# A nine-group Strassen output product: the turn of the next q in the following group's MLP phase, one subtraction on VectorE, second-half stores behind the turns of x

## The chip, the cores and the metric

The kernel runs on one core of a Trainium2 chip. The metric is the device time of one execution in microseconds (us); the smaller the better. TensorE is called PE, VectorE DVE, ScalarE ACT, GpSimd POOL and SyncE SP, as the profile names them. SP computes nothing here: it issues nearly all of the DMAs, in the order in which they are written.

## What is computed

Attention over 8 batches, 8 heads, 576 tokens and head size 64, with k and v averaged over blocks of 8 tokens (72 keys are left), and behind it an MLP on all 4608 tokens, 512 to 2048 to 512, with `g = h - tanh(h)` in the middle.

```python
k_p = k.reshape(B, H, Sp, pool, D).mean(axis=3)
v_p = v.reshape(B, H, Sp, pool, D).mean(axis=3)
scores = scale * np.matmul(q, k_p.transpose(0, 1, 3, 2))
attn = softmax(scores)                      # over the 72 pooled keys
attn_out = np.matmul(attn, v_p)
x = attn_out.transpose(0, 2, 1, 3).reshape(B * S, H * D)
h = x @ w_in
out = (h - np.tanh(h)) @ w_out
```

## The kernel before

The MLP goes over nine groups g = 0 to 8 of 512 tokens. Beside the MLP of group g runs the attention of batch nb = g + 1, and beside that the loading and pooling of batch nn = g + 2. A batch has 576 tokens, a group 512, so group g + 1 needs only the first blocks of batch g + 1: blocks 0 to 2 (of 128 tokens) for the groups 2 and 3, blocks 0 and 1 for the groups 4 and 5, block 0 for the group 6.

A group from 1 on has two phases. The **MLP phase** (lines 910 to 923) makes h for 16 slices of 128 hidden units from `xT`, the turned (transposed) x: eight matmuls for a pair of slices (`h_pair`, line 514), tanh of it on ACT (526), the difference to it on DVE (527, into `Gt`), and on DVE the sums `P`, `Q` that Strassen's scheme wants. The **product phase** (925 to 942) has seven products of eight steps each, in 14 half products u = 0 to 13 (line 562). They add up in two PSUM banks, C1 and C2, and `after_product` takes partial sums off: m4, m45, m451 are ACT copies of C1 at three points (594, 600, 607); POOL forms m4 - m45 (601) and m451 - m45 (608); DVE finishes with 605 and 610 into the output tile `O`. Between the half products stand the scores of batch nb (u = 0 to 4, line 333, exp on ACT, 352) and attention times values (`av`, u = 6, 7, 8, 9, 11, one block each: line 380 on PE, 397 and 398 on DVE into `x_sb`). SP then issues a DMA transpose that turns the block into `xT` (line 418).

At u = 7 POOL pools k (233 to 241, into `kd`) and v (251 to 275) of batch nn and casts q to `q_bf` (183, 187); then SP is given five DMA transposes that turn `q_bf` into `qT` (193). In the next MLP phase (p = 1 in group 1, p = 4 in later ones) SP turns `kd` into `kT` (316), POOL places that in `KB` (284 to 288), and SP issues the loads of the batch after (lines 137 to 170).

The order is written by hand (`tc.manual_schedule()`): each engine's instructions, and SP's DMAs, run in the order of the code, and an instruction that waits holds all that stand behind it on its engine. `store` (577) puts half a group's output on SP's queue: `store(g, 1)` behind product 5, `store(g, 0)` at the group's end.

Of the kernel before, what the change touches and what calls it, by code (L numbers as in the profile page):

```python
# [12 lines left out]
ALU = mybir.AluOpType  # L13
# [14 lines left out]
NG = T // TG  # L28
# [14 lines left out]
def kernel(  # L43
# [9 lines left out]
    nc = tc.nc  # L53
# [52 lines left out]
    m45 = const.tile([128, 2, HD], FP32, name="m45")  # L106
    m451 = const.tile([128, 2, HD], FP32, name="m451")
# [71 lines left out]
    def q_cast(b, eng=nc.gpsimd.tensor_copy, parts=1):  # L179
        t = q_raws.pop(b)  # L180
        n = H // parts
        for h in range(0, H, n):
            eng(  # L183
                out=q_bf[:, 0:R, h : h + n, :].rearrange("p j h d -> p h j d"),
                in_=t[:, h : h + n, 0:R, :],
            )
        eng(out=q_bf[:QT, R, :, :], in_=t[:QT, :, R, :])

    def q_dma_transpose(b):
        qT = work.tile([128, NHP, S], BF16, name="qT", tag="qT")  # L190
        for j in range(R + 1):
            rows = 128 if j < R else QT
            nc.sync.dma_start_transpose(  # L193
                out=qT[:, :, j * 128 : j * 128 + rows],
                in_=q_bf[:rows, j, :, :].rearrange("p h d -> p (h d)"),
            )
        qTs[b] = qT
# [84 lines left out]
    def kb_main(kb, ps, t0, t1, engs):  # L282
        kv = kb.rearrange("p (t x) -> p t x", x=KP)
        engs[0](out=kv[0:D, t0:t1, 0:G], in_=ps[0:D, :, 0:G])  # L284
        engs[1](out=kv[D:128, t0:t1, G:128], in_=ps[D:128, :, G:128])  # L285

    def kb_left(kb, ps, eng):
        eng(
            out=kb[D:128, :].rearrange("p (t x) -> p t x", x=KP)[:, :, 128 : 128 + LO],
            in_=ps[D:128, 0 : NM * LO].rearrange("p (x t) -> p t x", t=NM),  # L290
        )
# [22 lines left out]
    def k_dma_transpose(b):  # L314
        kT = work.tile([128, NT, 128], BF16, name="kT", tag="kT", bufs=1)
        nc.sync.dma_start_transpose(
            out=kT[:, :, :], in_=kdups.pop(b)[:, :, :, :].rearrange("p t a d -> p (t a d)")
        )
        kTs[b] = kT

    def k_place(b, eng):
        kT = kTs.pop(b)
        kb_main(KB[b % 2], kT[:, 0:NM, :], 0, NM, (eng, eng))
        kb_left(KB[b % 2], kT[:, NM, :], eng)
# [115 lines left out]
    def out_segments(c0, nrows):  # L440
        segs = []
        r = 0
        while r < nrows:
            c = c0 + r
            bb = c // S
            i = c % S
            if i < QA:
                j = i // 128
                p0 = i % 128
                ln = min(128 - p0, nrows - r, QA - i)  # L450
                dst = out[bb * S : bb * S + QA, :].rearrange("(p j) m -> p j m", j=R)[
                    p0 : p0 + ln, j, :
                ]
            else:
                ln = min(S - i, nrows - r)
                dst = out[bb * S + i : bb * S + i + ln, :]
            segs.append((r, r + ln, dst))
            r += ln
        return segs
# [62 lines left out]
    def h_pair(g, p, b0, ts):  # L522
        h_mms(g, p, PS[:, b0, :])
        h_mms(g, p + NP, PS[:, b0 + 1, :])
        t2 = TS[:, 2 * ts : 2 * ts + 2, :]
        nc.scalar.activation(out=t2, in_=PS[:, b0 : b0 + 2, :], func=ACT.Tanh)  # L526
        nc.vector.tensor_sub(out=Gt[:, p, :, :], in0=PS[:, b0 : b0 + 2, :], in1=t2)  # L527

    def h_one(g, p, s, b0, ts):
        h_mms(g, p + s * NP, PS[:, b0, :])  # L530
        nc.scalar.activation(out=TS[:, ts, :], in_=PS[:, b0, :], func=ACT.Tanh)
        nc.vector.tensor_sub(out=Gt[:, p, s, :], in0=PS[:, b0, :], in1=TS[:, ts, :])  # L532

    def sum_p(a, b):
        nc.vector.tensor_tensor(  # L535
            out=P[:, a:b, :], in0=Gt[:, a:b, 0, :], in1=Gt[:, a:b, 1, :], op=ALU.add
        )

    def sum_q(a, b):
        nc.vector.tensor_tensor(  # L540
            out=Q[:, a:b, :], in0=Gt[:, a:b, 0, 0:HT], in1=Gt[:, a:b, 1, HT:TG], op=ALU.add
        )

    def sum_d(a, b):
        nc.vector.tensor_tensor(  # L545
            out=Dg[:, a:b, :, :],
            in0=Gt[:, a:b, :, 0:HT],
            in1=Gt[:, a:b, :, HT:TG],
            op=ALU.subtract,
        )  # L550
# [8 lines left out]
    def product(bk, lhs, rhs, k0, k1, first):  # L559
        for k in range(k0, k1):  # L560
            for tt in range(2):
                nc.tensor.matmul(  # L562
                    PS[:, bk, tt * HD : (tt + 1) * HD],
                    lhsT=lhs(k, slice(tt * 128, (tt + 1) * 128)),
                    rhs=rhs[:, k, :],
                    start=(first and k == 0 and tt == 0),
                    stop=(k == NP - 1),
                    skip_group_check=True,
                )

    def chain(bk):
        return PS[:, bk, :].rearrange("p (t n) -> p t n", t=2)

    def store(g, th, tts=(0, 1), c0=0, c1=DM):
        for tt in tts:
            for n, (r0, r1, dst) in enumerate(out_segments(g * TG + th * HT + tt * 128, 128)):
                nc.sync.dma_start(out=dst[:, c0:c1], in_=O[r0:r1, 2 * th + tt, c0:c1])
# [14 lines left out]
    def after_product(g, n):  # L592
        if n == 0:
            nc.scalar.copy(out=m4, in_=chain(C1))
        if n == 1:
            nc.vector.tensor_tensor(out=O[:, 2:4, 0:HD], in0=chain(C2), in1=m4, op=ALU.add)
            sum_d(0, 2)
            sum_d(2, 4)
        if n == 2:
            nc.scalar.copy(out=m45, in_=chain(C1))  # L600
            nc.gpsimd.tensor_tensor(out=m4, in0=O[:, 2:4, 0:HD], in1=m45, op=ALU.subtract)  # L601
            sum_d(4, 6)
            sum_d(6, 8)
        if n == 3:
            nc.vector.tensor_tensor(out=O[:, 0:2, HD:DM], in0=m4, in1=chain(C2), op=ALU.subtract)
        if n == 4:
            nc.scalar.copy(out=m451, in_=chain(C1))
            nc.gpsimd.tensor_tensor(out=m451, in0=m451, in1=m45, op=ALU.subtract)  # L608
        if n == 5:
            nc.vector.tensor_tensor(  # L610
                out=O[:, 2:4, HD:DM], in0=m451, in1=chain(C2), op=ALU.subtract
            )
            store(g, 1)

    v_bf = (
        v_raw[0]
# [64 lines left out]
    for m, base, step, cm in (  # L681
# [6 lines left out]
            out=m,  # L688
# [7 lines left out]
    for i in range(2):  # L696
# [4 lines left out]
        out=spread.rearrange("p (t x) -> p t x", x=32)[:, :, 0:LO],  # L701
# [200 lines left out]
    def next_loads(b):  # L902
        load_k(b)
        load_v(b)
        load_q(b)

    for g in range(1, NG):
        nb = g + 1 if g + 1 < B else None
        nn = g + 2 if g + 2 < B else None
        for p in range(NP - 1):  # L910
            h_pair(g, p, (0, 2, 4, 6, 0, 2, 4)[p], p % 2)
            if p >= 4:
                sum_p(2 * p - 8, 2 * p - 6)
            if nb is not None and p == (1 if g == 1 else 4):
                k_dma_transpose(nb)
                k_place(nb, nc.gpsimd.tensor_copy)
                if nn is not None:
                    next_loads(nn)
        h_one(g, NP - 1, 1, 0, 2)
        h_one(g, NP - 1, 0, 1, 3)  # L920
        sum_p(6, 8)
        sum_q(0, 4)
        sum_q(4, 8)
        ps_a = Banks(2, 3, 4, 5, 0, 1)
        for u in range(14):
            n, half = u // 2, u % 2
            bk, lhs, rhs = products[n]
            if n == 6 and g == NG - 1:
                break
            product(bk, lhs, rhs, 4 * half, 4 * half + 4, n < 2)  # L930
            if half:
                after_product(g, n)
            if nb is not None:
                if u < NT:
                    scores(nb, u)
                if u in (6, 7, 8, 9, 11):
                    av(nb, (6, 7, 8, 9, 11).index(u), ps_b1, True)
                if u == 7 and nn is not None:
                    pool_k(nn, nc.gpsimd)
                    pool_v(nn, nc.gpsimd)  # L940
                    q_cast(nn)
                    q_dma_transpose(nn)
        if g < NG - 1:
            nc.scalar.copy(out=O[:, 0:2, 0:HD], in_=chain(C1))
            store(g, 0)
    store(NG - 1, 0, c0=HD)
    for tt, c0, c1, eng in (
        (0, 0, HD, nc.scalar.copy),
# [45 lines left out]
```

## Time and profile before

| | us |
|---|---|
| median of 3 runs | 382.73 (381.8 to 384.0) |
| the profiled execution | 385.25 |
| its span, first to last instruction | 383.5 |
| PE busy | 293.2 (76% of the span) |
| DVE, ACT, POOL busy | 221.6, 140.4, 139.1 |
| mean granted PE clock, as a share of full speed | 0.897 |

Times in rows are us from the span's start. The share of busy time is a mean over stages with different limits, so the stages have to be looked at one by one.

### The profile page before, as it was taken

What the parts mean: (1) busy time and instruction counts of PE and PEld (TensorE: products, weight loads), DVE (VectorE), ACT (ScalarE), POOL (GpSimd) and SP (SyncE); (2) the same over time, 40 slices, a digit from 0 to 9 for tenths busy, and PEclk for the clock granted to TensorE, in tenths of its full rate; (3) what the DMA queues carried; (4) which work ended last, traced back from release to release, by engine and by line L of the source; (5) the groups of instructions that cost most, each with busy time, mean ns of one, the idle gap of its engine ahead of it and who ended that gap; (6) DMA issues with size and microseconds to landing.
All of it is one profiled execution on the core that took longest, in us unless ns stands there. A gap on an engine that the chain in (4) does not pass through costs nothing.

```text
span 383.5 us, 5441 instructions
## 1 busy us (share of the span) xinstructions
PE 293.2 (76%) x2029; PEld 181.8 (47%) x2048; DVE 221.6 (58%) x389; ACT 140.4 (37%) x225; POOL 139.1 (36%) x126
## 2 busy tenths in 40 slices
PE   7899987699019991099944988199927899999991
PEld 2544553269004680045831476046812486485580
DVE  5766689686015970138903883249704875883860
ACT  4565730661004620036311642046212543623510
POOL 7307079207900079110593029701791111011030
PEclk9999999699758997579985999679986999999998
DMA  7999994921046920488103696158705505103004
GB/s 255 204 249 307 236 317 115 291 83 28 0 96 150 314 63 0 89 237 267 25 5 62 160 308 93 38 139 277 167 0 78 147 5 135 37 0 111 0 2 109
DMA packets 66538, 49.84 MB, mean 130 GB/s; under 512 B 40016, under 2 KB 53456, under 8 KB 66512
## 3 DMA queue, kind: packets, MB, share of 16 engines
q1 hardware_dynamic: 59104, 42.94, 42.5%
q0 software_dynamic: 4752, 4.72, 7.4%
q10 hardware_dynamic: 2656, 1.84, 1.8%
q8 instruction: 16, 0.26, 0.3%
q14 instruction: 10, 0.08, 0.1%
HBM read 36.70 MB, written 9.44 MB: 120 GB/s over the span
## 4 chain that ended last, share of the span: by engine, by line
PE 40%; POOL 23%; DVE 14%; DMA 10%; issue 4%; SPq 4%; ACT 3%; POOLq 0%; ACTq 0%; DVEq 0%
PE PS L514 19%; PE PS L562 14%; DVE Gt L527 6%; POOL v_raw L251 4%; POOL k_raw L233 4%; DMA w1b<-in_moe_w_in_dram 4%; SPq L193 3%; DMA k_raw<-in_k_dram 3%; DVE P L535 3%; ACT TS L526 2%; POOL q_bf L183 2%; PE PS L333 2%; DMA xT<-x_sb 2%; PE PS L496 2%; POOL k_raw L238 2%
## 5 line engine op out<-in xcount | busy, mean ns | idle before, releaser
L514 PE MATMUL PS<-xT,w1b 128*128 128x512 bf16 x496 | 124.7, 410 | 72.7 <-DMA xT<-x_sb 34.7
L514 PEld LDWEIGHTS <-w1b 128*128 128x128 f16 x512 | 53.0, 104 | 141.8 <-issue 54.7
L527 DVE TENSOR_TENSOR Gt<-PS,TS 128x1024 bf16<-128x1024 f32 x56 | 68.3, 1222 | 55.9 <-ACT TS L526 55.8
L526 ACT ACTIVATE TS<-PS 128x1024 f32<-128x1024 f32 x56 | 57.3, 1025 | 117.3 <-PE PS L514 116.7
L601 POOL TENSOR_TENSOR m<-O,m 128x512 f32<-128x512 f32 x8 | 10.9, 1366 | 111.9 <-DVE Dg L545 67.5
L610 DVE TENSOR_TENSOR O<-m,PS 128x512 f32<-128x512 f32 x8 | 5.5, 688 | 67.8 <-POOL m L608 67.2
L562 PE MATMUL PS<-w2b,Gt 128*128 128x256 f16 x256 | 33.6, 273 | 1.2 <-DVE Gt L532 1.0
L562 PE MATMUL PS<-w2b,P 128*128 128x256 f16 x256 | 32.3, 273 | 0.0
L398 DVE TENSOR_TENSOR x_sb<-PS,rden 128x256 bf16<-128x256 f32 x72 | 30.6, 425 | 2.5
L284 POOL COPY KB<-kT 64x288 bf16<-64x288 bf16 x6 | 2.8, 470 | 80.0 <-DMA kT<-kd 80.0
L233 POOL TENSOR_TENSOR k_raw<-k_raw 128x1280 f32<-128x1280 f32 x7 | 20.3, 2896 | 27.8 <-DMA k_raw<-in_k_dram 27.8
L562 PE MATMUL PS<-w2s,Dg 128*128 128x256 f16 x240 | 28.5, 273 | 0.0
L562 PEld LDWEIGHTS <-Gt 128*128 128x128 bf16 x256 | 24.3, 98 | 7.4 <-DVE Gt L532 2.9
L562 PEld LDWEIGHTS <-P 128*128 128x128 bf16 x256 | 24.6, 98 | 4.7 <-issue 1.4
L352 ACT ACTIVATE E<-PS 128x288 bf16<-128x288 f32 x60 | 21.4, 411 | 10.6 <-PE PS L333 10.6
L562 PEld LDWEIGHTS <-Dg 128*128 128x128 bf16 x240 | 23.0, 98 | 2.6 <-issue 0.2
L535 DVE TENSOR_TENSOR P<-Gt 128x1024 bf16<-128x1024 bf16 x32 | 22.1, 692 | 0.3
L545 DVE TENSOR_TENSOR Dg<-Gt 128x1024 bf16<-128x1024 bf16 x32 | 21.0, 719 | 0.0
L380 PE MATMUL PS<-VB,E 128*128 128x130 bf16 x240 | 20.2, 220 | 0.1
L333 PE MATMUL PS<-qT,KB 128*128 128x288 bf16 (+5 forms) x128 | 17.0, 289 | 2.4 <-POOL KB L285 2.3
L380 PEld LDWEIGHTS <-E 128*128 128x128 bf16 x240 | 16.8, 98 | 1.9 <-issue 0.4
L251 POOL TENSOR_TENSOR v_raw<-v_raw 128x1280 f32<-128x1280 f32 x6 | 17.3, 2881 | 0.0
(107 smaller groups left out, 353.0 us busy)
## 6 DMA issues: line engine op xcount, KB each, us to landing
k_raw<-in_k_dram SPq DMA_DIRECT2D x7, 1024.0 KB, 5.9
q_raw<-in_q_dram SPq DMA_DIRECT2D x7, 1024.0 KB, 9.9
v_raw<-in_v_dram SPq DMA_DIRECT2D x7, 1024.0 KB, 8.7
out_dram<-O SPq DMA_DIRECT2D x36, 128.0 KB, 2.4
out_dram<-O SPq DMA_DIRECT2D x16, 256.0 KB, 2.7
w1b<-in_moe_w_in_dram POOLq DMA_DIRECT2D x4, 512.0 KB, 15.0
w2b<-in_moe_w_out_dram POOLq DMA_DIRECT2D x4, 512.0 KB, 17.5
k_raw<-in_k_dram SPq DMA_DIRECT2D x7, 128.0 KB, 5.9
```

The costliest lines, as they stand in the source:

```text
L233: first = eng.tensor_tensor(out=r[:, :, 0:4, :], in0=r[:, :, 0:4, :], in1=r[:, :, 4:8, :], op=ALU.add)
L251: eng.tensor_tensor(out=r[:, :, 0:4, :], in0=r[:, :, 0:4, :], in1=r[:, :, 4:8, :], op=ALU.add)
L333: nc.tensor.matmul(dst[p : p + w], lhsT=KB[b % 2][:, o : o + w], rhs=qTs[b][:, m, c0:c1], start=True, stop=True,)
L352: nc.scalar.activation(out=E[:, t, half * hs : (half + 1) * hs], in_=ps[:, :], func=ACT.Exp, scale=SCALE)
L380: nc.tensor.matmul(ps[:, 2 * n : 2 * n + 2, :].rearrange("p h d -> p (h d)") if n < 2 else ps.rearrange("p (a s) d -> p a s d", s=2)[:, :, ...
L398: nc.vector.tensor_tensor(out=x_sb[:, half, :, :], in0=ps[:, :, 0:D], in1=rden[:, :, :].to_broadcast([128, 4, D]), op=ALU.mult,)
L514: nc.tensor.matmul(dst, lhsT=w1b[:, fb, i * 128 : (i + 1) * 128], rhs=xT[:, fb, c0 : c0 + TG], start=(fb == 0), stop=(fb == NFB - 1),)
L526: nc.scalar.activation(out=t2, in_=PS[:, b0 : b0 + 2, :], func=ACT.Tanh)
L527: nc.vector.tensor_sub(out=Gt[:, p, :, :], in0=PS[:, b0 : b0 + 2, :], in1=t2)
L535: nc.vector.tensor_tensor(out=P[:, a:b, :], in0=Gt[:, a:b, 0, :], in1=Gt[:, a:b, 1, :], op=ALU.add)
L545: nc.vector.tensor_tensor(out=Dg[:, a:b, :, :], in0=Gt[:, a:b, :, 0:HT], in1=Gt[:, a:b, :, HT:TG], op=ALU.subtract,)
L562: nc.tensor.matmul(PS[:, bk, tt * HD : (tt + 1) * HD], lhsT=lhs(k, slice(tt * 128, (tt + 1) * 128)), rhs=rhs[:, k, :], start=(first and k ...
```

## The change

Three edits. The five turns of q leave the end of the pooling block at u = 7 and stand in the next group's MLP phase, behind the turn of k (for g > 1; the first batch that is turned this way, 2, keeps its place ahead of the loop). The subtraction m451 - m45 goes from POOL to DVE. `store(g, 1)` moves from behind product 5 to behind u = 12, so behind the last turn of x; for the last group it stands behind the loop.

```diff
         if n == 4:
             nc.scalar.copy(out=m451, in_=chain(C1))
-            nc.gpsimd.tensor_tensor(out=m451, in0=m451, in1=m45, op=ALU.subtract)
+            nc.vector.tensor_tensor(out=m451, in0=m451, in1=m45, op=ALU.subtract)
         if n == 5:
             nc.vector.tensor_tensor(
                 out=O[:, 2:4, HD:DM], in0=m451, in1=chain(C2), op=ALU.subtract
             )
-            store(g, 1)
@@
             if nb is not None and p == (1 if g == 1 else 4):
                 k_dma_transpose(nb)
+                if g > 1:
+                    q_dma_transpose(nb)
                 k_place(nb, nc.gpsimd.tensor_copy)
                 if nn is not None:
                     next_loads(nn)
@@
                     pool_k(nn, nc.gpsimd)
                     pool_v(nn, nc.gpsimd)
                     q_cast(nn)
-                    q_dma_transpose(nn)
+            if u == 12:
+                store(g, 1)
         if g < NG - 1:
             nc.scalar.copy(out=O[:, 0:2, 0:HD], in_=chain(C1))
             store(g, 0)
+    store(NG - 1, 1)
     store(NG - 1, 0, c0=HD)
```

SP's queue from the product phase of group 1 to the loads in group 2, before (L193 turns q, L418 turns x, L577 stores, L316 turns k, L137 and L146 load k):

```order
L418 DMA_TRANSPOSE xT<-x_sb 128x4x128 x2
L193 DMA_TRANSPOSE qT<-q_bf 128x4x128 x4
L193 DMA_TRANSPOSE qT<-q_bf 128x4x64
L418 DMA_TRANSPOSE xT<-x_sb 128x4x128 x2
L577 DMA out_dram<-O 64x512 x4
L418 DMA_TRANSPOSE xT<-x_sb 128x4x64
L577 DMA out_dram<-O 64x512 x4
L316 DMA_TRANSPOSE kT<-kd 128x5x128
L137 DMA k_raw_86<-in_k_dram 128x4x512
L146 DMA k_raw_86<-in_k_dram 64x1x512
```

and the same stretch now:

```order
L418 DMA_TRANSPOSE xT<-x_sb 128x4x128 x4
L418 DMA_TRANSPOSE xT<-x_sb 128x4x64
L577 DMA out_dram<-O 64x512 x8
L316 DMA_TRANSPOSE kT<-kd 128x5x128
L193 DMA_TRANSPOSE qT<-q_bf 128x4x128 x4
L193 DMA_TRANSPOSE qT<-q_bf 128x4x64
L137 DMA k_raw_86<-in_k_dram 128x4x512
L146 DMA k_raw_86<-in_k_dram 64x1x512
```

All five turns of x now stand ahead of the turns of q, and the turns of q stand directly ahead of the loads. On POOL, before, the subtraction (L608, m_82 is m451) stood between the cast of q and the placing of k:

```order
L183 CAST q_bf<-q_raw 128x8x4x64
L187 CAST q_bf<-q_raw 64x512
L608 TENSOR_TENSOR m_82<-m_82,m_81 128x512
L284 COPY KB_91<-kT 64x4x72
L285 COPY KB_91<-kT 64x4x56
```

On DVE it now stands ahead of the fourth block of attention (L397, L398) of the same product phase:

```order
L398 TENSOR_TENSOR x_sb<-PS,rden 128x256
L608 TENSOR_TENSOR m_82<-m_82,m_81 128x512
L397 RECIPROCAL rden<-PS 128x4
L398 TENSOR_TENSOR x_sb<-PS,rden 128x256
L397 RECIPROCAL rden<-PS 128x4
L398 TENSOR_TENSOR x_sb<-PS,rden 128x256
L610 TENSOR_TENSOR O<-m_82,PS 128x2x256
```

L610, which reads it, no longer depends on POOL's queue.

## Rows read from the trace of the kernel before

**Rows 1.** Waits, whole span: engine line waited for, us in total, times, longest.
```profile
DVE O L610 <- POOL m L608: 67.2, 7, 12.7
...
PE PS L514 <- DMA xT<-x_sb: 34.7, 2, 17.4
...
PE PS L514 <- DVE x_sb L398: 29.2, 3, 9.7
```
**Rows 2.** Busy time by stretch: PE, PEld, DVE, ACT, POOL, clock, DMA share, GB/s.
```profile
144.80:162.20 17.40, 0.02 (x2) 0.01 (x1) 1.72 (x5) 0.59 (x1) 9.91 (x8) 0.58 0.21 41
162.20:179.00 16.80, 16.53 (x63) 7.01 (x66) 8.85 (x9) 7.67 (x8) 0.97 (x3) 0.82 0.94 266
...
321.20:335.00 13.80, 13.70 (x64) 6.27 (x65) 8.79 (x9) 8.23 (x9) 0.00 (x0) 1.00 0.34 83
```
**Rows 3.** Timeline of SP's queue: start us, us, what; groups 1, 2 and 4.
```profile
89.72 2.88 SPq L418 DMA_TRANSPOSE xT<-x_sb  x2
104.39 6.43 SPq L193 DMA_TRANSPOSE qT<-q_bf  x5
110.91 2.52 SPq L418 DMA_TRANSPOSE xT<-x_sb  x2
113.53 3.69 SPq L577 DMA_DIRECT2D out_dram<-O  x4
...
121.14 1.31 SPq L316 DMA_TRANSPOSE kT<-kd  x1
...
219.30 0.58 SPq L137 DMA_DIRECT2D k_raw<-in_k_dram  x1
```
**Rows 4.** Timeline of POOL, groups 0, 1 and 8; idle before in brackets.
```profile
65.56 1.72 POOL L257 TENSOR_TENSOR v_raw<-v_raw 128x320 f32<-128x320 f32 x1
...
88.11 1.27 POOL L601 TENSOR_TENSOR m<-O,m 128x512 f32<-128x512 f32 x1 [18.15 <-DVE Dg L545]
...
95.41 2.88 POOL L251 TENSOR_TENSOR v_raw<-v_raw 128x1280 f32<-128x1280 f32 x1
...
99.98 0.86 POOL L257 TENSOR_TENSOR v_raw<-v_raw 128x320 f32<-128x320 f32 x1
...
104.31 0.61 POOL L187 CAST q_bf<-q_raw 64x512 bf16<-64x512 f32 x1
...
368.24 1.96 POOL L601 TENSOR_TENSOR m<-O,m 128x512 f32<-128x512 f32 x1 [21.84 <-ACT m L600]
```
**Rows 5.** Timeline of PE, groups 1, 2 and 6.
```profile
80.24 1.04 PE L562 MATMUL PS<-w2b,Gt 128*128 128x256 f16 x8
81.11 0.41 PE L333 MATMUL PS<-qT,KB 128*128 128x288 bf16 x2
...
94.16 1.91 PE L562 MATMUL PS<-w2s,Dg 128*128 128x256 f16 x16
113.40 0.61 PE L514 MATMUL PS<-xT,w1b 128*128 128x512 bf16 x1 [17.33 <-DMA xT<-x_sb]
...
306.67 0.42 PE L333 MATMUL PS<-qT,KB 128*128 128x288 bf16 x2 [1.16 <-POOL KB L285]
```
**Rows 6.** Chain that ended last, in order of time, at group 1's last q turn.
```profile
109.62 1.20 SPq L193
```
**Rows 7.** Landing: page's DMA issues; then x's turn at 230.3 alone (ns min/median/max).
```profile
k_raw<-in_k_dram SPq DMA_DIRECT2D x7, 1024.0 KB, 5.9
...
qT<-q_bf SPq DMA_TRANSPOSE x30, 2.5
...
L418 SPq DMA_TRANSPOSE xT<-x_sb x1: 1234/1234/1234, 230.3 to 230.3; - x1
...
DMA to landing us min/median/max: 4.6/4.6/4.6
```
**Rows 8.** Timeline of DVE: last of block 3 in group 2; sums in group 8.
```profile
142.21 0.42 DVE L398 TENSOR_TENSOR x_sb<-PS,rden 128x256 bf16<-128x256 f32 x1
...
366.59 2.49 DVE L545 TENSOR_TENSOR Dg<-Gt 128x1024 bf16<-128x1024 bf16 x4
```

## The prediction

> **What bounds the kernel now.** I read the waits first, then the busy time by stretch, then the queues at the places that these two name. The waits [rows 1] show two stalls of one family. PE waits 34.7 us, in two pieces of 17.4, at the first h matmul of a group for turned x; and 29.2 us, three pieces of 9.7, for DVE to free a bank in line 398. DVE itself waits 67.2 us at line 610 for POOL's subtraction. The stretches [rows 2] show what such a stall costs twice: in the 17.4 us behind group 2's products PE is as good as idle, and the granted clock is 0.58 on the mean, so the lower of its two levels, 1.2 GHz, for most of it; the next MLP phase takes 16.8 us at 0.82, where group 7's, which follows its products without a gap, takes 13.8 at 1.00. So there are five stalls, behind groups 1 to 5, and each is also paid in clock.
>
> The queues say why. In group 1 POOL starts on line 601 at 88.11 and ends the cast of q at 104.9 [rows 4], 16.8 us later. SP has issued two turns of x by 92.6 and then stands at the turns of q until 104.39; these take 6.4 us to issue, and the other turns of x follow at 110.91 [rows 3]. Block 2 is needed for the next group, so PE, done at 96.07, starts at 113.40 [rows 5]. In groups 3 to 5 the needed blocks lie ahead of the turns of q, but line 608 stands behind the cast in POOL's queue, line 610 behind it in DVE's, and block 4's reciprocals and the next group's subtractions behind that.
>
> **The change, part by part.** *Turns of q.* Five issues of 6.4 us leave the place ahead of block 2's turn. In group 1 the third turn of x is then issued at 92.6 and lands 2.5 later, by the turns of q, which are the same instruction on the same shape [rows 7]: 95.1, before PE is done at 96.07. The 17.3 us stall goes. What is late next is the scores of the next group, since they need all of qT: their first step needs the last turn.
>
> Group 2 then starts at 96.07. With 13.8 us of MLP phase [rows 2] its products start at 109.9, and PE comes to the scores 0.87 later (80.24 to 81.11 [rows 5]), at 110.75. The turns of q cannot be earlier than now: the cast ends at 104.9, the last turn is issued at 109.62 [rows 6] and lands at about 111.9, taking 2.3 us for this half-size one (2.5 is the upper end). So PE waits 1.2 us, and I call 111.9 the time S of group 2.
>
> From there the loop is: S, the start of that first step's second half, lies 0.2 us behind the step's start, half of its 0.41, so at 81.3 in group 1, and line 601 starts at 88.11 [rows 4, 5]: 6.8 us. Line 601 to the last turn's landing is 111.9 - 88.11 = 23.8. One round: 30.6 us. PE's own round is 96.07 - 81.11 = 15.0 for the products behind the scores, 13.8 and 0.87: 29.6. So POOL's chain and the turns, not PE, set the pace, by 1.0 us.
>
> *Subtraction on DVE.* About 1.3 us go from POOL (line 601 is the same operation on the same shape [rows 4]), behind the cast, where nobody would now wait for them. It adds one f32 subtraction of 128x512 to DVE, ahead of block 3's reciprocals. Its price on DVE is about 0.6 us (a bf16 difference of twice as many elements takes 2.49/4 = 0.62 [rows 8]), an estimate, and twice that at the worst; block 3 is done at 142.63 in group 2 [rows 8] and its two banks are wanted at 144.8, so 2.2 us are covered. No row shows an f32 subtraction on DVE with both inputs in SBUF, beside POOL or alone. The nearest: line 601 took 1.96 us while DVE formed the differences Dg, and 1.27 otherwise [rows 4, 8], so the two hold each other up by about 0.7. Bounds: nothing for POOL, or 0.7 in each of five chains; and for DVE nothing, or a POOL instruction in flight of up to 2.88 [rows 4], which would be 0.7 or so beyond the cover. I take 0.7 on POOL and nothing beyond the cover, since rows 4 and 8 show just that pair at work.
>
> The Trainium skill has a rule for this (SBUF — State Buffer, "Who interferes with whom"): a DVE instruction with two SBUF inputs and a POOL instruction that reads SBUF exclude one another, and the second to start waits for the whole of the first. Rows 4 and 8 agree for a bf16 pair, no row shows the f32 one; by the rule the sum is the 315 below, without it 312.
>
> *Stores.* `store(g, 1)`'s four issues (3.7 us at most [rows 3]) come behind block 4's turn. Ahead of the turns of q SP now has block 4's turn (1.3), five to eight stores (0.9 each by the slowest row) and the turn of k (1.3). Block 4 is ready at S + 15.0 at the latest, when PE ends its products, so SP is free between S + 22.2 and S + 25.0; the cast frees the turns at S + 6.8 + 16.3 = S + 23.1 (88.11 to 104.39), or 23.8 with the 0.7. I take nothing; the bounds are 0 and 1.9 us a group, and 0 is nearer, since eight stores is the most that any group has.
>
> *Loads.* They stand behind the turns of q now, so they start 1.1 us ahead of S. POOL wants k 8 us behind S (6.8 and line 601), v 6 us later still (95.41 against 89.4 [rows 4]) and q last; k takes 5.9 to land [rows 7], so it is there at S + 5. I take nothing; the cover is 3 us.
>
> *Turns of x behind the loads.* In group 4 the loads started at 219.30, and the turn of x at 230.3 took 4.6 us to land instead of 2.5, at 234.9, 15.6 us behind the loads' start [rows 3, 7]. Now the loads start at S - 1.1 in groups 2 to 5, so block 0 lands at S + 14.5, blocks 1 and 2 at the spacing of SP's issues, 1.26 each, at 15.8 and 17.0. PE ends its products at S + 15.0. Group 3, which needs block 2, starts 2.0 us late: a round of 15.0 + 2.0 + 13.8 + 0.87 = 31.7. Groups 4 and 5, with two blocks, start 0.8 late: 30.5, which is hidden under the round that POOL sets. (The bounds are 2.5 us of landing, no cost at all, and the second rival.)
>
> **The sum.** S of group 2: 111.9 + 0.7 = 112.6. Four rounds lead to S of group 6, one of 31.7 and three of 30.6 + 0.7 = 31.3: 238.2. From there to the end nothing of weight changes: 383.5 - 306.67 = 76.8 [rows 5]. Span 315.0. The profiled execution was 1.75 longer than its span, so 316.8, and the median of the runs stands to it as 382.73 to 385.25: **315**. Without the 0.7 the span is 312.2 (111.9, 31.7, three of 30.6, 76.8), the time 312.
>
> **The rivals.**
>
> *PE alone sets the pace* (turns and POOL faster than I read): S of group 2 at 110.75, rounds of 29.6, span 306.0, time 306. Against it: the 16.8 us are POOL instructions back to back, and the 6.4 us are SP's own issue time.
>
> *The turns of x come late.* For it: the 4.6 us [rows 7] with loads on the queue; and now it is so in every group from 2 to 5. If each of these groups' followers starts 2.5 us late and the clock falls for a part of it (I take 15.3 for the MLP phase, midway between the 13.8 and 16.8 of rows 2), a round is 15.0 + 2.5 + 15.3 + 0.87 = 33.7: S of group 6 at 247.4, span 324.2, time 324. It decides from a start that is 1.6 us late. The Trainium skill (DMA: Bandwidth & Descriptors, "Queues, rings and completion order") says that one queue's descriptors are taken in ring order on each engine, so the turns wait for all that SP issued before; the 4.6 us agrees.
>
> *POOL is held up by DVE throughout: slower than before.* The pooling ran while DVE stood still at line 610; now it runs beside DVE's work. Line 257 took 1.72 us instead of 0.86 while DVE formed sums of weights [rows 4]. Were all of the 16.8 us doubled, S of group 2 would be 128.7, a round 47.4, the span 395, time 394. It decides from a stretch of 14.5 us a chain (five chains against the 72 us gained). Against it: line 251, 2.88 us at 95.41 [rows 4], and most of the chain are work of the MLP phase's first two thirds, where DVE has its reads from PSUM; the sums of two SBUF tensors that rows 4 and 8 show to hurt come behind the chain's end.
>
> *Only half works*: if the turns of x are still held by something in SP's queue, the two 17.3 us stalls stay and three of 9.7 go: 383.5 - 29.1 = 354, time 353.
>
> **How the numbers follow.** Forecast (310 to 319, with the bounds of the subtraction and the stores) 0.68, PE alone 0.10, turns of x late 0.17, half 0.03, POOL doubled 0.02. The range 306 to 325 leaves out the late end of the second rival, the last two and half of the first, in all less than 0.2. Faster by over 0.5%, which is about what can be told from no change, in all cases but the last: 0.97; slower 0.02; the same 0.01.
>
> **What would show it.** Right: no wait of line 514 for x over 2 us; no wait of line 610 for POOL; groups 2 to 6 at 31 us from scores to scores, with a wait of about 1 us for qT in line 333 at u = 0; PE's clock near 1.0 from group 2 on. Wrong: rounds of 33 or more with line 514 waiting for x (second rival); pooling rows longer than before by more than 1 us a chain (third); SP issuing the turns of q later than POOL's cast by more than 0.2 us (the store term).

## The result

The changed kernel takes 317.98 us (median of 4 runs, 316.82 to 319.41) against 382.68 before: a ratio of 0.831, 95% interval 0.8265 to 0.8353. The prediction was 315 with a range of 306 to 325; the span of the profiled execution is 315.1 us where the sum gave 315.0. That the two spans agree to 0.1 us is luck: two misses of some 3 us cancel, an opening that was 3.0 us shorter and rounds that were 3.3 us longer in sum.

The page of the changed kernel, its busy time and the granted clock in 40 slices:

```profile
PE 284.5 (90%) x2048; PEld 180.0 (57%) x2048; DVE 232.9 (74%) x397; ACT 140.5 (45%) x225; POOL 130.9 (42%) x118
...
PEclk9999999989999999999999997999999999999997
```

DVE's wait for POOL at line 610 [rows 1] is not among the waits any more. What is left around the MLP phase, from the waits of the changed kernel (us in total, times, longest):

```profile
PE PS L333 <- DMA qT<-q_bf: 5.7, 4, 2.1
...
PE PS L514 <- DVE x_sb L398: 5.0, 2, 3.4
DVE x_sb L398 <- DMA xT<-x_sb: 3.9, 2, 2.8
```

PE's timeline holds the whole course. These are, for the groups 2 to 6, the first matmul of the MLP phase (L514) and the first scores that had to wait for q (L333); group 5 has no wait there:

```profile
92.87 13.98 PE L514 MATMUL PS<-xT,w1b 128*128 128x512 bf16 x64
...
109.82 0.28 PE L333 MATMUL PS<-qT,KB 128*128 128x288 bf16 x1 [1.98 <-DMA qT<-q_bf]
...
124.72 13.97 PE L514 MATMUL PS<-xT,w1b 128*128 128x512 bf16 x64 [0.33 <-DMA xT<-x_sb]
...
141.76 0.30 PE L333 MATMUL PS<-qT,KB 128*128 128x288 bf16 x1 [2.07 <-DMA qT<-q_bf]
...
158.02 13.97 PE L514 MATMUL PS<-xT,w1b 128*128 128x512 bf16 x64 [1.68 <-DVE x_sb L398]
...
173.16 0.30 PE L333 MATMUL PS<-qT,KB 128*128 128x288 bf16 x1 [0.17 <-DMA qT<-q_bf]
...
191.10 15.66 PE L514 MATMUL PS<-xT,w1b 128*128 128x512 bf16 x64 [3.36 <-DVE x_sb L398]
...
207.47 0.41 PE L333 MATMUL PS<-qT,KB 128*128 128x288 bf16 x2
...
222.27 13.98 PE L514 MATMUL PS<-xT,w1b 128*128 128x512 bf16 x64
...
238.71 0.30 PE L333 MATMUL PS<-qT,KB 128*128 128x288 bf16 x1 [1.47 <-DMA qT<-q_bf]
```

Where before had an idle PE for twice 17.4 us and three times 9.7 [rows 1], there is nothing, 0.3, 1.7, 3.4 and nothing. From S to S (the second half of the first scores, so 207.67 in group 5) the rounds are 31.9, 31.4, 34.5 and 31.0 us; before, the five distances from group 1's scores to group 6's were 42 to 50. PE waits for q at the scores in four groups. The sum had four too, but not the same: it had none in group 3, which waited 2.1 us, and one of some 0.8 us in group 5, which had none. The third round is longer because the MLP phase behind group 4 starts 3.4 us late and then runs at the lower clock of 1.2 GHz for a while: the stretches (busy times, clock, DMA share, GB/s) of that phase and of the next group's, which started on time, are

```profile
191.10:206.60 15.50, 15.50 (x64) 6.67 (x65) 9.35 (x12) 7.66 (x8) 6.66 (x9) 0.89 0.57 134
222.30:236.10 13.80, 13.80 (x67) 6.26 (x65) 10.02 (x14) 8.24 (x9) 10.42 (x10) 1.00 0.56 132
```

The 1.7 us that the lower clock costs did not follow every such wait: in the experiments below, the same phase took 15.66 us behind a wait of 2.2 us (the subtraction from PSUM), and 13.97 behind one of 3.1 us (the cast first). What decides it was not tried.

The late start is the turn of x. The row names line 398, but that line itself waited for block 0's buffer, that is for the same turn. The issue (in ns) and the landing (in us) of block 0's turn behind the loads, in group 2 and then in group 4:

```profile
L418 SPq DMA_TRANSPOSE xT<-x_sb x1: 1257/1257/1257, 118.0 to 118.0; - x1
...
DMA to landing us min/median/max: 5.7/5.7/5.7
```

```profile
L418 SPq DMA_TRANSPOSE xT<-x_sb x1: 2598/2598/2598, 181.4 to 181.4; - x1
...
DMA to landing us min/median/max: 9.2/9.2/9.2
```

In group 3 it is 7.5 us, in group 5 3.6. [rows 7] had 4.6 for group 4 of before. That was not the only turn of x behind loads there: those of groups 2, 3 and 5, issued 16.0, 20.6 and 12.2 us behind the loads' start, took 2.6, 4.3 and 3.0 us, and the 4.3 came 6 us after the last load had landed. So the 4.6 us were no clean measure of what loads ahead of a turn cost.

The pace of the other rounds is POOL's chain and the turns. In group 1, line 183 is the part of the cast that the first four turns of q read; it ends at 101.69 and the turns start at 102.24:

```profile
99.80 1.89 POOL L183 CAST q_bf<-q_raw 128x2048 bf16<-128x2048 f32 x1
```

```profile
102.24 6.44 SPq L193 DMA_TRANSPOSE qT<-q_bf  x5
```

### The profile page after: what moved, and what is told of

It is laid out like the page before. It is cut to its first block, busy times and chain, and to the rows that moved or that the text cites. A ratio compares the mean times of both kernels' runs of the same rounds, so it can differ in the third digit from the quotient of the medians.

```text
span 315.1 us, 5444 instructions
## 1 busy us (share of the span) xinstructions
PE 284.5 (90%) x2048; PEld 180.0 (57%) x2048; DVE 232.9 (74%) x397; ACT 140.5 (45%) x225; POOL 130.9 (42%) x118
## 4 chain that ended last, share of the span: by engine, by line
PE 35%; POOL 22%; DMA 14%; DVE 13%; SPq 6%; issue 4%; ACT 2%; POOLq 0%; DVEq 0%; ACTq 0%
PE PS L562 18%; PE PS L514 9%; SPq L193 6%; DVE Gt L527 6%; DMA xT<-x_sb 4%; DMA w1b<-in_moe_w_in_dram 4%; POOL v_raw L251 4%; POOL k_raw L233 4%; DMA k_raw<-in_k_dram 3%; PE PS L333 3%; DMA qT<-q_bf 3%; PE PS L496 3%; POOL q_bf L183 2%; DVE w2b L553 2%; DVE P L535 2%
## 5 line engine op out<-in xcount | busy, mean ns | idle before, releaser
L514 PE MATMUL PS<-xT,w1b 128*128 128x512 bf16 x512 | 115.2, 386 | 12.3 <-DVE Gt L527 5.4
L514 PEld LDWEIGHTS <-w1b 128*128 128x128 f16 x512 | 50.5, 99 | 74.4 <-issue 14.2
L398 DVE TENSOR_TENSOR x_sb<-PS,rden 128x256 bf16<-128x256 f32 x72 | 30.6, 425 | 6.3 <-DMA xT<-x_sb 3.9
L233 POOL TENSOR_TENSOR k_raw<-k_raw 128x1280 f32<-128x1280 f32 x7 | 20.3, 2897 | 27.7 <-DMA k_raw<-in_k_dram 16.8
L333 PE MATMUL PS<-qT,KB 128*128 128x288 bf16 (+5 forms) x128 | 17.7, 289 | 5.8 <-DMA qT<-q_bf 5.7
L545 DVE TENSOR_TENSOR Dg<-Gt 128x1024 bf16<-128x1024 bf16 x32 | 22.0, 751 | 0.0
L380 PEld LDWEIGHTS <-E 128*128 128x128 bf16 x240 | 16.8, 98 | 1.9 <-issue 0.4
L607 ACT COPY m<-PS 128x512 f32<-128x512 f32 x8 | 4.7, 586 | 29.5 <-PE PS L562 29.5
L562 PE MATMUL PS<-w2s,Q 128*128 128x256 f16 x128 | 16.3, 273 | 0.0
```

Of the source, the lines that this page charges most:

```text
L233: first = eng.tensor_tensor(out=r[:, :, 0:4, :], in0=r[:, :, 0:4, :], in1=r[:, :, 4:8, :], op=ALU.add)
L333: nc.tensor.matmul(dst[p : p + w], lhsT=KB[b % 2][:, o : o + w], rhs=qTs[b][:, m, c0:c1], start=True, stop=True,)
L380: nc.tensor.matmul(ps[:, 2 * n : 2 * n + 2, :].rearrange("p h d -> p (h d)") if n < 2 else ps.rearrange("p (a s) d -> p a s d", s=2)[:, :, ...
L398: nc.vector.tensor_tensor(out=x_sb[:, half, :, :], in0=ps[:, :, 0:D], in1=rden[:, :, :].to_broadcast([128, 4, D]), op=ALU.mult,)
L514: nc.tensor.matmul(dst, lhsT=w1b[:, fb, i * 128 : (i + 1) * 128], rhs=xT[:, fb, c0 : c0 + TG], start=(fb == 0), stop=(fb == NFB - 1),)
L545: nc.vector.tensor_tensor(out=Dg[:, a:b, :, :], in0=Gt[:, a:b, :, 0:HT], in1=Gt[:, a:b, :, HT:TG], op=ALU.subtract,)
```

## The experiments

Ten runs follow. Times are compared with the changed kernel, which ran again in the first set at 318.52 us (316.97 to 319.31), and with the kernel before, at 383.3 to 383.6 beside them.

> The changed kernel once more, as the measure for the three beside it and for how much the opening (all ahead of group 1's products) varies: 77.2 us in the profile of the change, 80.2 in that of before. Time 318 +- 1.5.

It did: 318.52. Over the twelve profiles of this study the same opening code reaches group 1's products after 77.2 to 80.2 us, so 3 us of any comparison of two single profiles can be the opening.

**Each edit alone.** First the turns of q alone: the changed kernel with

```diff
-            nc.vector.tensor_tensor(out=m451, in0=m451, in1=m45, op=ALU.subtract)
+            nc.gpsimd.tensor_tensor(out=m451, in0=m451, in1=m45, op=ALU.subtract)
@@ n == 5
+            store(g, 1)
@@ u == 12, and behind the loop
-                store(g, 1)
-    store(NG - 1, 1)
```

> The first edit alone: the turns of q behind the turn of k in the next MLP phase; the subtraction stays on POOL and the stores behind product 5. Theory: line 610 then waits for POOL's whole chain as before (12 to 13 us in each of groups 1 to 5), DVE holds the bank of block 4 and the next group's subtractions, so each of the five rounds is about 42 us (before: 49, 50, 43, 42, 43) instead of 31: time 364 to 371. Rival: the turns of q alone were the stall, and the subtraction is a small matter: 318 to 325.

Measured: 366.4 us (one run). The waits of this kernel:

```profile
DVE O L610 <- POOL m L608: 67.2, 7, 12.7
PE PS L514 <- DVE x_sb L398: 47.4, 5, 9.7
```

The wait at line 610 is to the tenth what it was [rows 1], and PE now pays it in all five groups instead of three: 9.7 us at most, also where it had stood 17.4 for turned x. Then the subtraction alone: the kernel before with

```diff
-            nc.gpsimd.tensor_tensor(out=m451, in0=m451, in1=m45, op=ALU.subtract)
+            nc.vector.tensor_tensor(out=m451, in0=m451, in1=m45, op=ALU.subtract)
```

> The second edit alone: the subtraction on DVE, the turns of q and the stores where they were. Theory: the turns of x for block 2 still stand behind the turns of q, so the two 17 us stalls behind groups 1 and 2 stay; in groups 3 to 5 the wait of 9.7 us goes, but the turn of k still stands behind the turns of q, the rest of x and the stores in SP's queue, some 38 us behind the scores, and the next scores wait for it instead: nearly nothing is gained, 376 to 383. Rival, as in the prediction's last one: the three waits of 9.7 us go and nothing takes their place: 352 to 358.

Measured: 387.4 us (one run; the kernel before 382.1 to 385.2 beside it). Nothing is gained, and it lies a little above what was expected. PE's timeline and SP's queue at the end of group 3:

```profile
111.37 0.61 PE L514 MATMUL PS<-xT,w1b 128*128 128x512 bf16 x1 [17.64 <-DMA xT<-x_sb]
...
219.28 0.66 PE L333 MATMUL PS<-qT,KB 128*128 128x288 bf16 x2 [12.36 <-POOL KB L285]
```

```profile
200.91 6.41 SPq L193 DMA_TRANSPOSE qT<-q_bf  x5
207.41 2.52 SPq L418 DMA_TRANSPOSE xT<-x_sb  x2
...
215.65 1.32 SPq L316 DMA_TRANSPOSE kT<-kd  x1
```

The stall of 17.6 us for turned x is there, twice. Where DVE had held PE, PE now runs its MLP phase early and stands 12.4 us at the scores for KB: the turn of k is issued at 215.65, behind the turns of q, and nothing has moved that. So the gains do not add: 17 us for one edit, none for the other, 65 for both. Each takes away one of two waits that overlap, and PE then stands at the other one.

**The stores.** `store(g, 1)` behind product 5 again:

```diff
@@ n == 5
+            store(g, 1)
@@ u == 12, and behind the loop
-                store(g, 1)
-    store(NG - 1, 1)
```

> The change without its third edit: the stores of the second half stand behind product 5 again, ahead of block 4's turn. My theory: SP has the same issues to make by the time that the cast of q is done, line 610 no longer waits for POOL, and block 4 isn't needed for the next group, so the edit is worth nothing: within 1 us of the changed kernel (317 to 319). Rival: the stores ahead of block 4 hold SP up, and with it the turns of q: each round 1 to 2 us longer, 322 to 328.

Measured: 317.2 us (314.72 to 318.82). The ranges overlap: no difference is shown, so the third edit is worth nothing that these runs can tell. The one trace of this kernel has an opening 2.3 us longer than the changed kernel's, and only 0.5 us of wait where that has 3.4 (its turn of x in group 4 lands in 6.4 us); in the second profile of the changed kernel the wait is 3.0. Whether the third edit makes that turn later stays open.

**The late turns of x.** The load of q one group ahead:

```diff
         load_v(b)
-        load_q(b)
+        if b == 3:
+            load_q(b)
@@ u == 12
+                if g + 3 < B:
+                    load_q(g + 3)
                 store(g, 1)
```

> The loads of q leave the place behind the turns of q and stand one group earlier, behind the last turn of x (u = 12), so that only k and v (2.3 of 3.4 MB) are on the queue ahead of the turns of x. Theory: the late starts behind groups 2, 3 and 4 (0.3, 1.7 and 3.4 us, the last one paid again with 1.7 us at half clock) come from turns of x that wait for loads on the same queue; they go, the turns of x land in at most 4 us, and what is saved is what POOL's chain does not hide: 3 us in the round of groups 4 to 5, little elsewhere: 314 to 316. Rival: the turns land late for another reason (they hinder one another, or the traffic as such): no change, 317 to 319.

Measured: 328.4 us (326.2 to 329.8), 10 slower. The half of the theory that was to be tested held: with a third less on the queue ahead of them the turns of x land in 2.3 to 4.2 us, and line 514 has no wait for them. (They also stand further behind the loads, 10.7 to 10.9 us instead of 9.3; where other kernels below have all loads ahead at 10.8 to 11.2 us, block 0's turn takes 4.5 to 5.1, and here 2.5 to 4.1.) The other half fell. The loads of q now stand ahead of the turns of q instead of behind them, and SP's queue, PE's scores and POOL's cast in group 1 and 2 read

```profile
97.29 1.26 SPq L170 DMA_DIRECT2D q_raw<-in_q_dram  x1
98.61 0.64 SPq L162 DMA_DIRECT2D q_raw<-in_q_dram  x1
99.29 6.48 SPq L577 DMA_DIRECT2D out_dram<-O  x8
105.86 1.27 SPq L316 DMA_TRANSPOSE kT<-kd  x1
107.24 6.82 SPq L193 DMA_TRANSPOSE qT<-q_bf  x5
```

```profile
101.70 1.89 POOL L183 CAST q_bf<-q_raw 128x2048 bf16<-128x2048 f32 x1
```

```profile
112.36 0.28 PE L333 MATMUL PS<-qT,KB 128*128 128x288 bf16 x1 [2.75 <-DMA qT<-q_bf]
115.28 0.42 PE L333 MATMUL PS<-qT,KB 128*128 128x288 bf16 x1 [2.63 <-DMA qT<-q_bf]
```

Line 183 is done at 103.6, the turns start at 107.24: SP is 3.6 us late, and PE waits for it. Over the five groups it is 3.6, 0.8, 2.1, 2.0 and 0 us late, 8.5 in all, where the changed kernel has some 2.7. The rest of the 10 us lies between S and line 601, 8.0 to 8.2 us in groups 2 to 4 instead of 6.6, since the scores now wait for q in two places. So in the changed kernel SP's issue time, beside POOL's chain, was within a hair of setting the pace, which the next runs test.

**POOL's chain against SP's queue.** Cast before pooling v, and nothing else:

```diff
                     pool_k(nn, nc.gpsimd)
-                    pool_v(nn, nc.gpsimd)
                     q_cast(nn)
+                    pool_v(nn, nc.gpsimd)
```

> POOL casts q ahead of pooling v (nothing else moves). Theory of the prediction: POOL's chain and the turns set the pace; the cast is done 6 us earlier. If POOL's chain were the only thing, PE's own round of 29.6 us would set the pace: some 6 us less, 311 to 313. My theory now, from the changed kernel's trace: SP is busy with turns of x, stores and the turn of k until 0.5 us behind the cast in groups 1, 3 and 4 and only 2 us ahead of it in group 2, so SP's queue takes over: 1 to 3 us less, 315 to 317.

Measured: 314.9 us (314.1 to 316.3), 3.6 less, at the better edge of what SP's theory allowed. The rows (POOL's cast, then SP) show why not more:

```profile
95.17 1.89 POOL L183 CAST q_bf<-q_raw 128x2048 bf16<-128x2048 f32 x1
```

```profile
97.87 5.62 SPq L577 DMA_DIRECT2D out_dram<-O  x8
103.59 1.26 SPq L316 DMA_TRANSPOSE kT<-kd  x1
104.96 6.42 SPq L193 DMA_TRANSPOSE qT<-q_bf  x5
```

That part of the cast is ready 7.9 us before SP comes to the turns.

**A new order on SP.** The cast first, and the turns of k and q and the loads at the end of the same group:

```diff
@@ p == 1 or 4: in group 1 alone
-                k_dma_transpose(nb), q_dma_transpose(nb), next_loads(nn)
@@ u == 12
+                if nn is not None:
+                    k_dma_transpose(nn)
+                    q_dma_transpose(nn)
                 store(g, 1)
+                if g + 3 < B:
+                    next_loads(g + 3)
```

> The cast of q ahead of pooling v as in the run before, and in SP's queue the turn of k and the turns of q directly behind the last turn of x of the same group (u = 12), then the second half's stores, then the loads of the batch after next but one, then the first half's stores. Theory: turns of q land about 5 us before the scores want them, the loads start 5 us earlier and are over when the turns of x are issued; no wait for qT in line 333 and no late start of line 514: PE alone sets the pace, rounds of 29.6 us: 302 to 306. Rival: the engines beside PE (DVE at 26 of 29.6 us) or the DMAs in a denser schedule hold it above 31: 314 to 318.

Measured: 331.3 us (329.1 to 333.6): neither of the two. Every wait that it was to remove is gone, and a new one stands in the product phase, here on DVE and PE in group 2:

```profile
124.25 0.69 DVE L605 TENSOR_TENSOR O<-m,PS 128x512 f32<-128x512 f32 x1 [6.85 <-DMA out_dram<-O]
```

```profile
124.99 3.57 PE L562 MATMUL PS<-w2s,Dg 128*128 128x256 f16 x16 [5.05 <-DVE O L605]
```

The first half's stores had slid behind the loads; line 605 writes `O` again and waits until the store of the group before has read it. SP's queue was the wrong place to look for room by moving things about.

**What the subtraction costs.** Line 608 took 1.85 us on DVE in group 1, not 0.6, and line 241 beside it on POOL 1.87 instead of 1.54. To tell whether that is the two reading SBUF at once:

```diff
-            nc.scalar.copy(out=m451, in_=chain(C1))
-            nc.vector.tensor_tensor(out=m451, in0=m451, in1=m45, op=ALU.subtract)
+            nc.vector.tensor_tensor(out=m451, in0=chain(C1), in1=m45, op=ALU.subtract)
```

> The subtraction m451 - m45 on DVE reads C1 in PSUM itself; the ACT copy of C1 (line 607) goes. Theory: the 1.69 to 1.85 us that line 608 takes on DVE, and the 0.33 us by which line 241 on POOL grew (1.54 to 1.87), are the two holding each other up because both read two SBUF tensors; with one input in PSUM line 608 takes 0.7 and line 241 1.54 again. It is worth 0.3 us in each of five chains, at most 1.5 us in all: 316 to 318. Rival: the lengths are the price of an f32 subtraction as such: line 608 stays above 1.2 and line 241 at 1.87, time unchanged.

Measured: 315.4 us (314.2 to 316.6), 3.1 less. The groups of the changed kernel, then of this one (its line 607 is the same subtraction), with busy us and mean ns:

```profile
L241 POOL TENSOR_TENSOR kd<-k_raw 128x640 bf16<-128x640 f32 x7 | 12.4, 1773 | 0.6
L608 DVE TENSOR_TENSOR m<-m,m 128x512 f32<-128x512 f32 x8 | 11.2, 1398 | 2.1 <-ACT m L607 1.8
```

```profile
L241 POOL TENSOR_TENSOR kd<-k_raw 128x640 bf16<-128x640 f32 x7 | 10.8, 1540 | 0.5
L607 DVE TENSOR_TENSOR m<-PS,m 128x512 f32<-128x512 f32 x8 | 5.5, 684 | 0.5 <-PE PS L562 0.5
```

Line 608 falls from 1398 ns to 684 and line 241 is back at 1540, with the same arithmetic on the same shape: the two did hold each other up. The mean of 1398 hides two kinds. In groups 1 to 5, beside POOL's pooling, line 608 takes 1.69 to 1.85 us, and in groups 6 to 8, where POOL has nothing to pool, 0.69 with both inputs in SBUF:

```profile
249.75 0.69 DVE L608 TENSOR_TENSOR m<-m,m 128x512 f32<-128x512 f32 x1
```

The trace of before had this price already: in its opening, with POOL idle, DVE adds two f32 tensors of the same shape in SBUF.

```profile
9.09 0.69 DVE L233 TENSOR_TENSOR k_raw<-k_raw 128x512 f32<-128x512 f32 x1 [2.07 <-DMA k_raw<-in_k_dram]
```

The edit also takes away ACT's copy of C1 (586 ns on the mean) ahead of the subtraction. That the whole gains 3 us, twice the expectation, goes with blocks 3 and 4 being ready over 1 us earlier, so that SP is too; it was not separated further.

**Both, and fewer issues on SP.** The last two edits together; and with them the second half's stores on ACT's queue:

```diff
             if u == 12:
-                store(g, 1)
+                store(g, 1, eng=nc.scalar)
```

> The two small gains together: the cast of q ahead of pooling v, and the subtraction m451 - m45 read from C1 in PSUM. Theory: SP's queue sets the pace in most rounds now (its turns of q come up to 7 us behind the cast when the cast is early), and what the PSUM subtraction gives back is mostly block 4 and its turn 1.3 us earlier, that is SP free earlier; so the two add up only in part: 312 to 315. Rival: POOL's chain was the pace and both shorten it, the gains add up or more and PE alone is left: 306 to 310.

Measured: 312.3 us (308.7 to 314.3), within the theory's range. It is 6.2 us less, where the two alone gave 3.6 and 3.1, so these runs do not tell whether they add up in part or in full.

> As the kernel beside it (cast first, subtraction from PSUM), and the second half's stores of groups 1 to 7 are issued from ACT's queue instead of SP's. Theory: that takes 2.5 us of issues out of SP's queue ahead of the turns of q in each of groups 1 to 5; turns and loads come that much earlier, the loads are over sooner before the turns of x, and the round falls to PE's own 29.6 to 30.2 us: 303 to 308. Rival: DMA traffic or ACT (its copies and tanh behind a store that waits) takes over, no gain over the kernel beside it: 312 to 316.

Measured: 305.9 us (304.7 to 308.6), a ratio of 0.799 to the kernel before (0.793 to 0.805): 12 us faster than the changed kernel, 6 faster than the one beside it. SP's queue in group 1 and PE's first scores in groups 2 to 4:

```profile
95.81 3.02 SPq L577 DMA_DIRECT2D out_dram<-O  x4
98.93 1.27 SPq L316 DMA_TRANSPOSE kT<-kd  x1
100.31 6.43 SPq L193 DMA_TRANSPOSE qT<-q_bf  x5
```

```profile
108.35 0.41 PE L333 MATMUL PS<-qT,KB 128*128 128x288 bf16 x2
...
138.10 0.41 PE L333 MATMUL PS<-qT,KB 128*128 128x288 bf16 x2
...
167.59 0.41 PE L333 MATMUL PS<-qT,KB 128*128 128x288 bf16 x2
```

The rounds are 29.7 and 29.5 us and nothing waits in them: that is PE's own round, which the prediction had put at 29.6. The loads start earlier in the round too, and no turn of x makes PE wait. (Later, PE waits once more for q, 0.3 us in group 5.)

## Why the prediction was right, and where it was not

*The stall and its two causes*: right. Both waits went, and the two runs with one edit each show that both had to. The rival "only half works" was wrongly built, though: it put down 29 us of gain to the subtraction alone, and the run shows none, since the turn of k behind the turns of q was next at that place. Its chance was small; its price should have been found by asking once more what is late next.

*The start*: group 2's scores were put at 112.6 and came at 109.82. The opening was 3.0 us shorter in this execution (77.2 against 80.24), which has nothing to do with the change. Counted from group 1's scores (81.3 before, 78.3 now), the step is 31.3 forecast and 31.5 measured. Inside it two terms trade places: POOL's chain grew by 0.3 us instead of 0.7, and SP came 0.5 us late instead of 0.

*The rounds*: 31.7 and three of 31.3, in sum 125.6; measured 31.9, 31.4, 34.5, 31.0, in sum 128.9. Three of four are right to 0.3, but not always for the reason given. The 31.7 was to be PE starting 2.0 us late for turned x; that start was 0.3 us late, and the 31.9 measured is POOL's chain and the turns of q, the first of which took 2.3 us to issue instead of 1.2. That the two agree is luck. In the second round both paths end within 0.2 us of each other. Three of the prediction's own marks also went against it: a wait of line 514 for x of over 2 us, one round above 33, and SP later than the cast by more than 0.2. The terms:

- *Subtraction*: 0.7 on POOL was forecast, 0.33 measured; 0.6 on DVE forecast, 1.69 to 1.85 measured in the five groups that count. That is above the first bound named (twice the price, 1.2) and inside the second (waiting for a POOL instruction in flight, 2.88). The price alone, 0.69, could have been read from line 233 in the opening of before, shown above. The rule of the Trainium skill that was weighed there (SBUF — State Buffer, "Who interferes with whom") holds for the f32 pair too: 1.69 to 1.85 us beside POOL's pooling, 0.69 without it, and 684 ns beside it with one input in PSUM.
- *Stores and the rest of SP's queue*: 0 was taken out of 0 to 1.9. SP came to the turns of q 0.5, 0, 0.5, 1.6 and 0 us behind line 183 in the five groups. That is inside the bounds, but the reading behind it was too narrow: POOL's chain and SP's queue are of nearly the same length, and to take 7 us off POOL's alone was worth 3.6.
- *Turns of x behind the loads*: this is the term that was mis-sized. One row was carried over to all groups, block 0 landing 15.6 us behind the loads' start and the others 1.26 apart, with starts 2.0, 0.8, 0.8 and 0 us late; they were 0.3, 1.7, 3.4 and 0. Block 0 landed 15.0, 16.8 and 18.6 us behind that start in groups 2 to 4, and three turns that had been held up landed within 0.9 us (group 2: 123.7, 124.1, 124.6), not 2.5. In the third round the clock fell on top. By its own mark, a start 1.6 us late, the second rival came true in two starts of four; by its price, in one. The mechanism, that turns land late behind loads, is borne out by the run with fewer loads ahead of them; the size came from a single row, in which the turn stood 11.0 us behind the loads and not 9.3.

*The end*: 76.8 forecast, 315.1 - 238.71 = 76.4 measured. *From the span to the time*: the ratio of the profiled execution of before to its median was carried over, 0.6% downward; here the profiled execution was the fastest of four, so the median came out 3 us above the forecast, 1.2 of it above the profiled execution.

What stays open: why the turn of x lands later from group 2 to group 4, 5.7, 7.5, 9.2 us, though the loads start 1.1 us ahead of S each time. The loads of q themselves land later from group to group (9.6, 10.5, 11.3 us at most), the last of them 14.4, 14.9 and 15.7 us behind the loads' start. That is 1.3 of the 3.6 us by which the turn falls back; it lands 0.6, 1.9 and 2.9 us behind that last load. Neither part was tried.

## What to carry to other kernels

When two engines wait in one place, ask of each edit what it gains alone: here none and 17 us, together 65, because each wait hid behind the other. A queue that issues DMAs is an engine with a busy time of its own: sum up its issues for a round and set them beside the other engines' rounds before anything is moved onto it or about in it. A wait read from one row of the trace gives a mechanism, not a size: the 4.6 us became 3.6 to 9.2.

## What the runs showed of the hardware

Issue time on SP is dear: a DMA transpose mostly holds it for 1.2 to 1.3 us (2.9 at most), a store for 0.6, so that the issues from group 1's first turn of x on add up to 23 of a round of 31 us, and with the waits for blocks of x between them SP is taken up for 28. To move the second half's stores to ACT's queue, four issues in group 1, was worth 6 us in all. The Trainium skill (DMA: Bandwidth & Descriptors, "Issuing engines are not separate DMA queues") calls the issue time usually small beside the DMA itself; for these, of 2.3 to 2.8 us from issue to landing, it is a quarter to a half. And an f32 subtraction of 128x512 on DVE with both inputs in SBUF took 1.69 to 1.85 us beside POOL's pooling, 0.69 without it, and 0.68 beside it with one input in PSUM.
